# Seven block products for eight in the up-projection of a spectral layer with a feed-forward block

## The chip, the core and the metric

The kernel runs on one core of one Trainium2 chip. The metric is the device time of one execution in microseconds (us), as the median of a few runs on one chip. The engines are named as in the profile: PE is the matrix engine (PEld its weight loads), DVE the vector engine, ACT the scalar engine, POOL the GpSimd engine, SP the engine that issues the DMAs.

## The reference

Two stages, eight batches of 3008 rows and 256 columns, all in fp32:

```python
X = np.fft.rfft(x, axis=1)                       # x: 8 x 3008 x 256
Yr = Xr @ w_r - Xi @ w_i + b_r                   # Xr, Xi: real and imaginary part of X
Yi = Xr @ w_i + Xi @ w_r + b_i
Y  = shrink(Yr) + 1j * shrink(Yi)                # sign(v) * max(|v| - 0.01, 0)
y  = np.fft.irfft(Y, n=3008, axis=1)             # then y as 24064 rows of 256
h  = y @ w_in                                    # 256 -> 2048
out = (h - np.tanh(h)) @ w_out                   # 2048 -> 256
```

## The kernel before

**Number format.** Every matrix operand is split into a high part, rounded to a short mantissa by an ACT cast, and a low part, the fp32 remainder, which DVE subtracts. A product is then three matmuls: high by high, high by low, low by high. These operands have the type fp32r in the program and take one pass. A few matmuls of the transforms have plain fp32 operands and take two passes each, so that the trace counts them twice.

**The spectral stage** works batch by batch. `Forward` multiplies pairs of 94 rows by the first DFT factor (`dft`, L215 to L217), and `keep` copies the result out for a DMA to `a_dram`. `Spectrum` loads it again and applies the second factor (`transform`, L264), the complex product with the weights (`product`, L284, 256 columns wide), the shrinking, and the first factor of the inverse transform (L319 to L321), which goes to `z_dram`.

**The feed-forward stage** works on chunks of `CP = 5` pairs, that is 470 columns (rows of y). `Chunk.time` applies the last inverse factor (L407, 94 columns per pair) and splits its result into `yh` and `yl`. For each of 16 tiles f of 128 features there is then one step:

```python
h   = 6 matmuls: (win_l, yh), (win_h, yh), (win_h, yl), two halves of 256 each   # up, L420
th  = tanh(h)          # ACT,  L423
g   = h - th           # DVE,  L425
gh  = round(g)         # ACT,  L427
gl  = g - gh           # DVE,  L433
o0, o1 += 6 matmuls: (wout_l, gh), (wout_h, gh), (wout_h, gl) for each half      # down, L445
```

The two result banks `o0` and `o1` collect over the 16 steps; `store` copies them out and sends them. There are 52 chunks: 50 of 470 columns and two of 282 at the end. Before the first FFN matmul, batch 0 goes through a special start. The first `FIRST = 3` chunks are interleaved while the fp64 weights `w_in` and `w_out` are converted.

**The order** is written out by hand: every engine runs its instructions in the order of the program. The up matmuls of step g + 2 (`AHEAD = 2`) stand ahead of the down matmuls of step g. The spectral stage of the next batch is put into slots, one slot per step, by `plan_forward`, `plan_spectrum` and `put`; `run(g)` issues what stands in slot g. All DMAs are issued by SP. GpSimd does one subtraction in the whole program (`w2`, L118). PSUM has eight banks of 512 fp32 columns: two for `h`, two for `o`, four (`ps_f`) for the rest.

Of the kernel before, what the change touches and what calls it, by code (L numbers as in the profile page):

```python
# [66 lines left out]
def spectral_ffn(ctx, tc, x, w_r, w_i, b_r, b_i, w_in, w_out, f1, f2, i1, i2, out):  # L67
# [4 lines left out]
    CP = 5  # L72
    CT = CP * 94
# [6 lines left out]
    cvt = ctx.enter_context(tc.tile_pool(name="cvt", bufs=2))  # L80
    ffn = ctx.enter_context(tc.tile_pool(name="ffn", bufs=3))
    dram = ctx.enter_context(tc.tile_pool(name="dram", bufs=2, space=bass.MemoryType.DRAM))
    ps_h = ctx.enter_context(tc.tile_pool(name="ps_h", bufs=2, space=PSUM))
    ps_o = ctx.enter_context(tc.tile_pool(name="ps_o", bufs=1, space=PSUM))
    ps_f = ctx.enter_context(tc.tile_pool(name="ps_f", bufs=4, space=PSUM))

    def split(src, name, pool=const, tag=None, bufs=None, rest=nc.vector):
        hi = pool.tile(list(src.shape), F32R, name=f"{name}_h", tag=f"{tag or name}_h", bufs=bufs)
        lo = pool.tile(list(src.shape), F32R, name=f"{name}_l", tag=f"{tag or name}_l", bufs=bufs)
        nc.scalar.copy(out=hi, in_=src)  # L90
        rest.tensor_tensor(out=lo, in0=src, in1=hi.bitcast(F32), op=ALU.subtract)  # L91
        return hi, lo

# [10 lines left out]
    def linear_loads():  # L104
        wr = ffn.tile([P, 2, D], F32, name="wr_f", tag="g_h")
        wi = load.tile([P, 2, D], F32, name="wi_f", tag="at", bufs=3)
        bias = const.tile([P, 2, D], F32, name="bias")
        yield wr, wi, bias
        for k, v in enumerate((b_r, b_i)):
            yield nc.sync.dma_start(out=bias[:, k, :], in_=v.rearrange("(o e) -> o e", o=1).to_broadcast([P, D]))  # L110
        yield nc.sync.dma_start(out=wi, in_=w_i.rearrange("(t p) e -> p t e", p=P))
        yield nc.sync.dma_start(out=wr, in_=w_r.rearrange("(t p) e -> p t e", p=P))

    def combine_linear(wr, wi, bias, zero):
        w2 = ffn.tile([P, 2, D], F32, name="w2_f", tag="g_h")
        w3 = ffn.tile([P, 2, D], F32, name="w3_f", tag="g_h")
# [30 lines left out]
    def split_f64(part, k, raw):  # L147
# [36 lines left out]
    class Forward:  # L184
# [4 lines left out]
        def load(self):  # L189
            if self.ch == 0:  # L190
                a_dram[self.b] = dram.tile([NP, 96, D], F32, name=f"a_{self.b}", tag="a")
            pool, tag = (load, "xt")
            if self.b == 0:
                pool, tag = ((load, "xt"), (load, "zin"), (work, "yh"), (work, "yl"))[self.ch // 2]
            self.xt = pool.tile([96, XC, D], F32, name="xt", tag=tag)
            nc.sync.dma_start(out=self.xt, in_=x[self.b, :, self.ch * XC:(self.ch + 1) * XC, :])

        def split(self, q, homes=None):
            src, name = self.xt[:94, 2 * q:2 * q + 2, :], f"x_{self.b}_{self.ch}_{q}"
            if homes is None:  # L200
                self.x[q] = split(src, name, work, "sp", 3)
                return
            hi, lo = (
                pool.tile(list(src.shape), F32R, name=f"{name}_{part}", tag=tag, bufs=bufs)
                for part, (pool, tag, bufs) in zip("hl", homes)
            )
            nc.scalar.copy(out=hi, in_=src)
            nc.vector.tensor_tensor(out=lo, in0=src, in1=hi.bitcast(F32), op=ALU.subtract)
            self.x[q] = hi, lo

        def dft(self, q):
            xh, xl = self.x[q]
            self.ps[q] = ps_f.tile([P, 512], F32, name="ps_f1", tag="f")
            pv = self.ps[q][:96].rearrange("p (a d) -> p a d", d=D)
            nc.tensor.matmul(pv, f1h, xl, start=True, stop=False)  # L215
            nc.tensor.matmul(pv, f1l, xh, start=False, stop=False)  # L216
            nc.tensor.matmul(pv, f1h, xh, start=False, stop=True)  # L217
# [26 lines left out]
    class Spectrum:  # L244
        def __init__(self, b, jp):
            self.b, self.jp = b, jp
# [10 lines left out]
        def transform(self):  # L257
            ps = self.ps = ps_f.tile([P, 512], F32, name="ps_f2", tag="f")
# [7 lines left out]
        def dft(self):  # L266
            self.transform()
            ps = self.ps
            self.xh = work.tile([P, 2, 2, P], F32R, name="xh", tag="sp_h", bufs=3)
            self.xl = work.tile([P, 2, 2, P], F32R, name="xl", tag="sp_l", bufs=3)  # L270
# [5 lines left out]
            nc.vector.tensor_tensor(out=self.xl.rearrange(flat), in0=ps, in1=self.xh.bitcast(F32).rearrange(flat), op=ALU.subtract)  # L276
            nc.vector.tensor_tensor(out=xi, in0=pr[:, :, 0, :], in1=xi, op=ALU.add)
# [9 lines left out]
        def cross(self, k):  # L287
            if k == 0:
                self.vv = ps_f.tile([P, 512], F32, name="ps_v", tag="f")
                self.product(self.vv[:, :D], self.xh[:, :, 1], self.xl[:, :, 1], lin[2])  # L290
            else:
                self.product(self.vv[:, D:], self.xh[:, :, 0], self.xl[:, :, 0], lin[1])

        def shared(self):
            t1 = ps_f.tile([P, 512], F32, name="ps_t1", tag="f")
            self.product(t1[:, :D], *self.s, lin[0])
            tb = self.temp("tb", "th")
            nc.vector.tensor_tensor(out=tb, in0=t1[:, :D].unsqueeze(1).to_broadcast([P, 2, D]), in1=bias, op=ALU.add)
# [16 lines left out]
        def inverse(self):  # L315
            zh, zl = self.z
            pz = ps_f.tile([P, 512], F32, name="ps_i1", tag="f")
            pzv = pz.rearrange("p (j e) -> p j e", j=2)
            nc.tensor.matmul(pzv, i1h, zl, start=True, stop=False)  # L319
            nc.tensor.matmul(pzv, i1l, zh, start=False, stop=False)  # L320
            nc.tensor.matmul(pzv, i1h, zh, start=False, stop=True)  # L321
# [7 lines left out]
    class WholeSpectrum(Spectrum):  # L329
        def temp(self, name, tag):  # L330
            return ffn.tile([P, 2, D], F32, name=name, tag=tag)

        def dft(self):
            self.transform()
            self.xf = work.tile([P, 2, 2, P], F32, name="xf", tag="sp_h", bufs=3)
# [37 lines left out]
        def inverse(self):  # L373
            self.pz = ps_f.tile([P, 512], F32, name="ps_i1", tag="f")
            nc.tensor.matmul(self.pz.rearrange("p (j e) -> p j e", j=2), i1f, self.mn, start=True, stop=True)

    total = B * NP
    sizes = [CP] * (total // CP)
    if total % CP:
        sizes = sizes[:-1] + [(CP + total % CP + 1) // 2, (CP + total % CP) // 2]  # L380
    begin = [sum(sizes[:c]) for c in range(len(sizes))]
    NCH = len(sizes)

    FIRST = 3

    class Chunk:
        def __init__(self, c):
            self.c, self.n = c, sizes[c] * 94
            self.pairs = [(p // NP, p % NP) for p in range(begin[c], begin[c] + sizes[c])]

        def load(self):
            self.zt = load.tile([96, CP, D], F32, name="zin", tag="zin")
            k = 0
            while k < len(self.pairs):
                b, p = self.pairs[k]
                n = sum(q[0] == b for q in self.pairs[k:])
                nc.sync.dma_start(out=self.zt[:, k:k + n, :], in_=z_dram[b][p:p + n].rearrange("a p d -> p a d"))
                k += n

        def time(self, t):  # L400
            n = self.n
            if t == 0:
                tags = ("st", "st") if self.c == FIRST - 1 else ("yh", "yl")
                self.yh, self.yl = (work.tile([P, 2, 512], F32R, name=m, tag=g) for m, g in zip(("yh", "yl"), tags))
            ps = ps_f.tile([P, 512], F32, name="ps_i2", tag="f")
            for k, (_, p) in enumerate(self.pairs):
                nc.tensor.matmul(  # L407
                    ps[:, k * 94:(k + 1) * 94], self.zt[:, k, t * P:(t + 1) * P], i2t[:, p * 94:(p + 1) * 94],
                    start=True, stop=True,
                )  # L410
            nc.scalar.copy(out=self.yh[:, t, :n], in_=ps[:, :n])  # L411
            nc.vector.tensor_tensor(out=self.yl[:, t, :n], in0=ps[:, :n], in1=self.yh[:, t, :n].bitcast(F32), op=ALU.subtract)

        def up(self, f):
            n = self.n
            h = ps_h.tile([P, 512], F32, name="h", tag="h")
# [304 lines left out]
```

## Time and profile before

| | |
|---|---|
| median of 3 runs | 2696.31 us (2693.75 to 2697.34) |
| span of the profiled execution, first to last instruction | 2694.1 us |
| granted PE clock, mean of the span | 0.998 |
| PE busy | 2676.7 us, 99% |
| DVE busy | 1748.3 us, 65% |
| ACT busy | 1377.5 us, 51% |
| POOL busy | 2.0 us, 0% |
| HBM traffic | 60 GB/s over the span |

The time of the profiled execution is its span of 2694.1 us and a little around it; the median of the runs is 2.2 us above the span. In a timeline a row shows the start of a group of equal instructions, the time from the start of its first to the end of its last, and the idle time before it with what ended it. Matmuls overlap, since the next one enters while the last drains: what one costs in a stream is the distance from its start to the next start, not its duration.

### The profile page before, as it was taken

The numbers are of one execution on the slowest core, as the hardware profiler recorded it, in microseconds if no ns is written. First come the engines' busy times: TensorE is split into PE (matmuls) and PEld (weight loads), VectorE is DVE, ScalarE is ACT, GpSimd is POOL, SyncE is SP. The second block draws the span as 40 slices with busy tenths as digits, with TensorE's granted clock in tenths as the row PEclk, the third lists the DMA queues.
The fourth block names the chain that finished last, engine by engine and source line by source line (L and its number), as shares of the span: only waits on it lengthen the run. The fifth ranks groups of instructions, "written<-read, shape, count | busy, mean of one in ns | idle before, by whom it ended". The sixth has DMA issues, their size and how long they took to land.

```text
span 2694.1 us, 36955 instructions
## 1 busy us (share of the span) xinstructions
PE 2676.7 (99%) x14169; PEld 2391.6 (89%) x14169; DVE 1748.3 (65%) x3079; ACT 1377.5 (51%) x2587; POOL 2.0 (0%) x5
## 2 busy tenths in 40 slices
PE   8999999999999999999999999999999999999999
PEld 6788988999889998999988999899988999998989
DVE  6895786666557666566755667666665666655555
ACT  5555555454554446454455445644455444444445
POOL 0000000000000000000000000000000000000000
PEclk9999999999999999999999999999999999999999
DMA  6423223110231103111022110411113111100000
GB/s 196 141 75 106 65 83 109 46 54 26 69 90 43 50 32 111 57 47 46 24 81 80 46 46 31 118 56 50 39 39 108 50 39 41 35 23 22 20 20 17
DMA packets 105135, 163.47 MB, mean 61 GB/s; under 512 B 7488, under 2 KB 70976, under 8 KB 104864
## 3 DMA queue, kind: packets, MB, share of 16 engines
q1 hardware_dynamic: 104960, 161.13, 19.8%
q8 instruction: 111, 1.82, 0.3%
q14 instruction: 64, 0.52, 0.1%
HBM read 86.13 MB, written 74.97 MB: 60 GB/s over the span
## 4 chain that ended last, share of the span: by engine, by line
PE 94%; DVE 3%; DMA 1%; ACT 1%; issue 1%; SPq 0%; DVEq 0%; ACTq 0%
PE o L445 37%; PE h L420 37%; PE ps_v L284 4%; PE ps_i L407 4%; PE ps_f L264 3%; PE ps_t L284 2%; PE ps_f L215 1%; PE ps_f L217 1%; PE ps_f L216 1%; PE ps_v L352 1%; DVE g L425 1%; PE ps_i L320 1%; PE ps_i L321 1%; PE ps_i L319 1%; DVE gl L433 0%
## 5 line engine op out<-in xcount | busy, mean ns | idle before, releaser
L425 DVE TENSOR_TENSOR g<-h,th 128x470 f32<-128x470 f32 (+1 forms) x832 | 532.2, 640 | 540.0 <-ACT th L423 531.9
L423 ACT ACTIVATE th<-h 128x470 f32<-128x470 f32 (+1 forms) x832 | 463.9, 558 | 757.3 <-PE h L420 756.3
L433 DVE TENSOR_TENSOR gl<-g,gh 128x470 fp32r<-128x470 f32 (+1 forms) x832 | 531.9, 639 | 285.8 <-ACT gh L427 203.2
L427 ACT CAST gh<-g 128x470 fp32r<-128x470 f32 (+1 forms) x832 | 483.0, 581 | 408.6 <-DVE g L425 401.2
L445 PE MATMUL o<-gh,wout_l 128*128 128x470 f32 (+1 forms) x1664 | 631.3, 379 | 1.1 <-ACT gh L427 1.1
L445 PE MATMUL o<-gl,wout_h 128*128 128x470 f32 (+1 forms) x1664 | 616.1, 370 | 1.1 <-DVE gl L433 1.1
L445 PE MATMUL o<-gh,wout_h 128*128 128x470 f32 (+1 forms) x1664 | 615.8, 370 | 0.0
L420 PE MATMUL h<-yl,win_h 128*128 128x470 f32 (+1 forms) x1664 | 480.7, 370 | 0.0
L420 PE MATMUL h<-yh,win_l 128*128 128x470 f32 (+1 forms) x1664 | 480.1, 370 | 0.0
L420 PE MATMUL h<-yh,win_h 128*128 128x470 f32 (+1 forms) x1664 | 479.5, 369 | 0.0
L445 PEld LDWEIGHTS o<-gl,wout_h 128*128 128x128 f32 x1664 | 312.8, 188 | 40.8 <-DVE gl L433 2.1
L445 PEld LDWEIGHTS o<-gh,wout_l 128*128 128x128 f32 x1664 | 313.1, 188 | 35.1 <-ACT gh L427 1.7
L420 PEld LDWEIGHTS h<-yh,win_l 128*128 128x128 f32 x1664 | 310.5, 188 | 36.2 <-ACT yh L411 0.4
L420 PEld LDWEIGHTS h<-yl,win_h 128*128 128x128 f32 x1664 | 310.6, 188 | 35.5
L420 PEld LDWEIGHTS h<-yh,win_h 128*128 128x128 f32 x1664 | 310.6, 188 | 35.5
L445 PEld LDWEIGHTS o<-gh,wout_h 128*128 128x128 f32 x1664 | 313.5, 188 | 32.0
L309 DVE TENSOR_TENSOR y<-tb,ps_v 64x256 f32<-64x256 f32 x384 | 160.2, 417 | 12.0 <-ACT tb L356 6.8
L407 PEld LDWEIGHTS ps_i<-i,zin 96*128 96x128 f32 x1024 | 126.1, 192 | 5.0 <-DVE st L231 1.0
L407 PE MATMUL ps_i<-i,zin 96*128 96x94 f32 x1024 | 128.0, 272 | 1.0 <-DVE st L231 0.8
L91 DVE TENSOR_TENSOR x_l<-xt,x_h 94x512 fp32r<-94x512 f32 x126 | 85.6, 686 | 46.2 <-ACT x_h L90 44.3
L264 PEld LDWEIGHTS ps_f<-f,at 128*128 128x128 f32 x768 | 101.5, 192 | 13.6 <-issue 8.2
L264 PE MATMUL ps_f<-f,at 128*128 128x128 f32 x768 | 103.1, 277 | 5.7 <-DMA at<-a 5.7
(98 smaller groups left out, 2077.8 us busy)
## 6 DMA issues: line engine op xcount, KB each, us to landing
xt<-in_x SPq DMA_DIRECT2D x64, 384.0 KB, 3.6
at<-a SPq DMA_DIRECT2D x96, 256.0 KB, 2.8
z<-zo SPq DMA_DIRECT2D x96, 256.0 KB, 2.0
out<-ot SPq DMA_DIRECT2D x50, 470.0 KB, 2.9
a<-st SPq DMA_DIRECT2D x56, 384.0 KB, 3.2
zin<-z SPq DMA_DIRECT2D x44, 480.0 KB, 4.2
w_raw<-in_moe_w_in SPq DMA_DIRECT2D x8, 512.0 KB, 4.6
w_raw<-in_moe_w_out SPq DMA_DIRECT2D x8, 512.0 KB, 5.1
```

Of the source, the lines that this page charges most:

```text
L91: rest.tensor_tensor(out=lo, in0=src, in1=hi.bitcast(F32), op=ALU.subtract)
L215: nc.tensor.matmul(pv, f1h, xl, start=True, stop=False)
L264: nc.tensor.matmul(pv[:, t, jj], self.at[:, jj, t * P:(t + 1) * P], rhs, start=True, stop=True)
L284: nc.tensor.matmul(dst, lhs[:, t], rhs[:, t, :], start=n == 0, stop=n == 5)
L309: nc.vector.tensor_tensor(out=y[ri * 64:(ri + 1) * 64, jj, :], in0=common(jj, ri), in1=self.vv[jj * 64:(jj + 1) * 64, ri * D:(ri + 1) * D] ...
L407: nc.tensor.matmul(ps[:, k * 94:(k + 1) * 94], self.zt[:, k, t * P:(t + 1) * P], i2t[:, p * 94:(p + 1) * 94], start=True, stop=True,)
L420: nc.tensor.matmul(h[:, :n], lhs[:, t, f * P:(f + 1) * P], rhs[:, t, :n], start=k == 0, stop=k == 5)
L423: nc.scalar.activation(out=th[:, :n], in_=h[:, :n], func=AF.Tanh)
L425: nc.vector.tensor_tensor(out=g[:, :n], in0=h[:, :n], in1=th[:, :n], op=ALU.subtract)
L427: nc.scalar.copy(out=gh[:, :n], in_=g[:, :n])
L433: nc.vector.tensor_tensor(out=gl[:, :n], in0=g[:, :n], in1=gh[:, :n].bitcast(F32), op=ALU.subtract)
L445: nc.tensor.matmul(self.o[t][:, :n], lhs[:, f, t * P:(t + 1) * P], rhs[:, :n], start=f == 0 and k == 0, stop=f == NF - 1 and k == 2,)
```

## The change

From chunk 3 on (`FIRST`), the up-projection takes two tiles f at once. The weights of the pair are seen as a 2x2 matrix of blocks A (two halves of the 256 inputs by two tiles f), the chunk's y as a 2x2 matrix of blocks B (two halves of the inputs by two halves of the columns), and the product is made with Strassen's seven block products in Winograd's order, not eight. Each block product is three matmuls (high and low parts as before) on half a chunk's columns: 21 matmuls for a pair of tiles where there were 12 on a whole chunk. Besides:

- Chunks have 512 or 480 columns (`widths`), six to a batch, so that 48 chunks replace 52, and the halves have 256 or 240.
- The sums of weight blocks (`sums`, three tiles in high and low parts; a fourth overwrites one block of `win`) are made once, in slots 36 to 53 (`weight_sums`). The sums of y blocks (`t1` to `t4`) are made per chunk: differences on GpSimd (`Chunk.sums`), then seven casts on ACT and seven subtractions on GpSimd (`operands`). The operand tiles have one buffer each.
- The sums of products are made in PSUM. A pair has two banks, `H0` or `H1`: `c11` and `acc` in one, `c21` and `c22` in the other. `keep` has ACT copy `c11` to the tile `p7` (in `late`) and then `acc` to `c11`; `u3` and `low_right` have DVE add `p7` to `acc`. PE waits for each of these, since they touch a bank that it writes next.
- tanh, g, gh and gl work on both tiles at once, 1024 columns (960) wide.
- The remainders of the spectral stage's splits (`x_l`, `s_l`, `z_l`) go from DVE to GpSimd; the product with the low part comes last in their matmuls.
- y is copied raw from PSUM by ACT (`take`), with a spill tile where a chunk border cuts a pair; `Unit` loads and transforms it in pieces of two or three pairs.
- The slots, the tiles' homes and the PSUM banks are laid out anew; the early steps (chunks 0 to 2) keep the six matmuls of `up`, now 512 wide.

In this diff the loop at the end is the new order of the main part; one turn is two slots and one pair of tiles.

```diff
+    widths = [512, 512, 512, 512, 480, 480]
+    def split_into(hi, lo, src, rest=nc.gpsimd):
         nc.scalar.copy(out=hi, in_=src)
         rest.tensor_tensor(out=lo, in0=src, in1=hi.bitcast(F32), op=ALU.subtract)
...
+        def sums(self, k):                        # Chunk
+            b11, b12, b21, b22 = self.halves()
+            sub = lambda o, a, b: nc.gpsimd.tensor_tensor(out=o, in0=a, in1=b, op=ALU.subtract)
+            if k == 0:
+                sub(self.spare(0), b22, b12)
+                sub(b12, b12, b11)
+            elif k == 1:
+                sub(self.spare(1), b22, b12)
+            else:
+                sub(self.spare(0), b21, self.spare(1))
...
+    class Pair:
+        def product(self, dst, left, right, start=False):
+            ah, al = self.left(left)
+            bh, bl = (v[:, :self.m] for v in ys[right])
+            for k, (a, b) in enumerate(((al, bh), (ah, bh), (ah, bl))):
+                nc.tensor.matmul(dst, a, b, start=start and k == 0, stop=k == 2, skip_group_check=True)
+        def phase0(self):
+            self.open()
+            self.product(self.c11, "s3", "t3", True)
+            self.product(self.acc, "a11", "b11")
+        def keep(self):
+            nc.scalar.copy(out=self.p7, in_=self.c11)
+            nc.scalar.copy(out=self.c11, in_=self.acc)
+        def phase1(self):
+            self.product(self.acc, "s2", "t2")
+            self.product(self.c11, "a12", "b21")
+        def u3(self):
+            nc.vector.tensor_tensor(out=self.c21, in0=self.acc, in1=self.p7, op=ALU.add)
+        def phase2(self):
+            self.product(self.acc, "s1", "t1")
+        def low_right(self):
+            nc.vector.tensor_tensor(out=self.c22, in0=self.acc, in1=self.p7, op=ALU.add)
+        def phase3(self):
+            self.product(self.acc, "a21", "b22")
+            self.product(self.c21, "a22", "t4")
...
+        for Q in range(-1, PERIODS + 2):
+            call(Q, "low_right")
+            call(Q - 1, "high")
+            run_later()
...
+            call(Q - 2, "down", 1, 0)
+            call(Q - 1, "low")
+            call(Q + 1, "phase0")
+            call(Q + 1, "keep")
+            run_last()
+            run(sa)
+            run_later()
...
+            call(Q, "phase3")
+            call(Q, "tanh")
+            run_last()
+            call(Q - 2, "down", 1, 1)
...
+            call(Q + 1, "phase1")
+            call(Q + 1, "u3")
+            call(Q, "g")
+            call(Q - 1, "down", 0, 0)
+            run(sb)
+            call(Q - 1, "down", 0, 1)
+            call(Q + 1, "phase2")
```

The order of the built program shows this in three places. On PE before, in the middle of the main part, up (L420) and down (L445) alternate, six matmuls each:

```order
L420 MATMUL h<-yh,win_l 128x470 x2
L420 MATMUL h<-yh,win_h 128x470 x2
L420 MATMUL h<-yl,win_h 128x470 x2
L445 MATMUL o_15868<-gh,wout_l 128x470
L445 MATMUL o_15868<-gh,wout_h 128x470
L445 MATMUL o_15868<-gl,wout_h 128x470
```

On PE after, in the main part near the end of the program, from `phase0` of one pair on (`y_t` and `y_b` are operands t and b, `y_more` holds b22 and t4, `sum` the weight sums):

```order
L576 MATMUL H_2035<-y_t_1981,sum_1_1848 128x256
L576 MATMUL H_2035<-y_t_1981,sum_0_1847 128x256 x2
L576 MATMUL H_2035<-y_b_1982,win_l 128x256
L576 MATMUL H_2035<-y_b_1982,win_h 128x256 x2
L576 MATMUL H_2036<-y_more,win_l 128x256
L576 MATMUL H_2036<-y_more,win_h 128x256 x2
L576 MATMUL H_2036<-y_more,win_l 128x256
L576 MATMUL H_2036<-y_more,win_h 128x256 x2
L505 MATMUL o_25267<-gh,wout_l 128x512
L505 MATMUL o_25267<-gh,wout_h 128x512
L505 MATMUL o_25267<-gl,wout_h 128x512
L576 MATMUL H_2035<-y_t_1984,sum_1_1846 128x256
```

The up matmuls now stand in four groups (`phase0`, `phase3`, `phase1`, and `phase2` further on), with the pair's other bank or one half of a down between those that wait for each other.

On ACT before, a stretch of the main part:

```order
L427 CAST gh<-g 128x470
L423 ACTIVATE th<-h 128x470
L427 CAST gh<-g 128x470
L423 ACTIVATE th<-h 128x470
```

On ACT after, in the last chunks of the main part, with four of the next chunk's operand casts:

```order
L614 CAST gh<-th 128x1024
L584 COPY late<-H_2035 128x256
L585 COPY H_2035<-H_2035 128x256
L607 ACTIVATE th<-H_2036 128x1024
L87 CAST y_t_1981<-late 128x240
L87 CAST y_b_1982<-raw 128x240
L87 CAST y_t_1984<-late 128x240
L87 CAST y_b_1983<-raw 128x240
L614 CAST gh<-th 128x1024
```

The two copies of `keep` come between the cast of one pair and the tanh of the next, and the operand casts ahead of the next cast. On GpSimd, where before there was one subtraction, the operands' differences and remainders stand between those of the spectral stage:

```order
L531 TENSOR_TENSOR late<-raw 128x256
L531 TENSOR_TENSOR raw<-raw 128x256
L88 TENSOR_TENSOR z_0_l<-mn,z_0_h 128x512
L531 TENSOR_TENSOR late<-raw 128x256
L88 TENSOR_TENSOR y_t_1981<-late,y_t_1981 128x256
L88 TENSOR_TENSOR y_b_1982<-raw,y_b_1982 128x256
```

So one remainder of the spectral stage (`z_0_l`) is ahead of a chunk's operands in GpSimd's queue.

More of the change, by code (lines that the diff above doesn't have):

```diff
@@ L373, in inverse @@
         def inverse(self):
-            self.pz = ps_f.tile([P, 512], F32, name="ps_i1", tag="f")
+            self.pz = bank("ps_i1")
             nc.tensor.matmul(self.pz.rearrange("p (j e) -> p j e", j=2), i1f, self.mn, start=True, stop=True)
[L377 to L382, printed above, removed]
-    FIRST = 3
+    widths = [512, 512, 512, 512, 480, 480]
@@ L386, in spectral_ffn @@
+    Unit.turn = 0
     class Chunk:
         def __init__(self, c):
[L388 to L398, printed above, removed]
@@ L400, in time @@
-        def time(self, t):
-            n = self.n
[L402 to L412, printed above, removed]
@@ L461, in spectral_ffn @@
-    slots = {}
-    def put(slot, fn, *a):
-        slots.setdefault(slot, []).append((fn, a))
-    def plan_forward(b, start, each, ahead, first=0):
-        for ch in range(first, NP // XC):
-            f = Forward(b, ch)
-            put(start + ch * each - ahead, f.load)
-            for q in range(XC // 2):
-                put(start + ch * each + q * each // 2, f.part, q)
-    def plan_spectrum(b, start, each, ahead, lag):
+            th, gh, gl = (v[i % 4 // 2][:, i % 2, :n] for v in early_tiles)
@@ new lines, in plan_spectrum, with plan_forward, calmest, prepare @@
+            if shared == cross:
+                busy(k + shared, 9.0)
+    def plan_forward(f, q, slot):
+        put(slot - 1, 2, f.split, q)
+        put(slot, 7, f.part, q)
+        busy(slot, 0.8)
+        busy(slot - 1, 0.1)
+    def calmest(lo, hi, n, us):
+        found = sorted(sorted(range(lo, hi + 1), key=lambda k: (load_at.get(k, 0.0), k))[:n])
+        for k in found:
+            busy(k, us)
+        return found
+    def prepare(c):
+        chunk = chunks[c]
+        at = zero_slot(c)
+        if c > FIRST:
+            put(at - 15, 0, chunk.unspill)
+        put(at - 5, 9, chunk.sums, 0)
+        put(at - 4, 9, chunk.sums, 1)
+        put(at - 3, 1, chunk.operands, "t3", "b11", "t2", "b21")
+        put(at - 2, 1, chunk.operands, "t1")
+        put(at - 2, 9, chunk.sums, 2)
+        put(at - 1, 1, chunk.operands, "b22", "t4")
+        busy(at - 3, 1.0)
+        busy(at - 1, 0.6)
@@ L689, in spectral_ffn, with rise, finish, fall @@
-    for g in range(HELD, len(order)):
-        step(g, lambda: run(g))
+        ready, half = {}, {}
+        def rise(g):
+            if g < len(order):
+                c, f = order[g]
+                half[g] = chunks[c].up(f, g)
+        def finish(g):
+            if g in half:
+                c, f = order[g]
+                ready[g] = chunks[c].rest(*half.pop(g))
+        def fall(g, t):
+            if g in ready:
+                c, f = order[g]
+                chunks[c].down(f, *ready[g], t)
```

593 lines of the change are left out of this document (421 added, 172 removed).

## The prediction

> **What bounds the kernel now.** I read the page's first lines first, then PE's own waits, then a table by stage, and last the timeline of PE, to learn what a matmul costs in a stream.
>
> ```profile
> span 2694.1 us, 36955 instructions
> PE 2676.7 (99%) x14169; PEld 2391.6 (89%) x14169; DVE 1748.3 (65%) x3079; ACT 1377.5 (51%) x2587; POOL 2.0 (0%) x5
> PE 94%; DVE 3%; DMA 1%; ACT 1%; issue 1%; SPq 0%; DVEq 0%; ACTq 0%
> ```
>
> PE is busy for 99% of the span and carries 94% of the chain that ended last. From the waits of PE, longest first, and the busy time by stage (us, then PE, PEld, DVE, ACT, POOL with counts, granted clock, DMA):
>
> ```profile
> PE ps_f L264 <- DMA at<-a: 5.7, 1, 5.7
> PE o L445 <- ACT gh L427: 1.1, 1, 1.1
> 270.00:2690.00 2420.00, 2419.21 (x12977) 2179.04 (x12976) 1549.68 (x2715) 1224.80 (x2307) 0.00 (x0) 1.00 0.18 53
> ```
>
> PE waits for almost nothing, and in the main part it is busy for 2419 of 2420 us at full clock. So the time is the sum of the distances between matmul starts. A change pays what it takes out of that sum, less the new waits that it makes. These groups hold the FFN (count, busy, mean ns):
>
> ```profile
> L445 PE MATMUL o<-gh,wout_l 128*128 128x470 f32 x1600 | 612.6, 383 | 1.1 <-ACT gh L427 1.1
> L420 PE MATMUL h<-yh,win_h 128*128 128x470 f32 x1600 | 466.1, 373 | 0.0
> L420 PE MATMUL h<-yh,win_h 128*128 128x282 f32 x64 | 13.3, 289 | 0.0
> ```
>
> Each of the six groups (three of up, three of down) has 1600 matmuls of 470 columns and 64 of 282. Their mean of 370 to 380 ns is no price, because matmuls overlap. The timeline of PE gives it, from start to start:
>
> ```profile
> 1504.72 0.58 PE L420 MATMUL h<-yl,win_h 128*128 128x470 f32 x2
> 1505.14 0.39 PE L319 MATMUL ps_i<-z_l,i_h 128*128 128x512 f32 x1
> ...
> 1505.83 0.38 PE L445 MATMUL o<-gh,wout_l 128*128 128x470 f32 x1
> ...
> 1507.10 0.58 PE L420 MATMUL h<-yh,win_l 128*128 128x470 f32 x2
> ...
> 1508.37 0.40 PE L284 MATMUL ps_v<-w_h,xl 128*128 128x256 f32 x2
> ...
> 1509.08 0.38 PE L445 MATMUL o<-gh,wout_l 128*128 128x470 f32 x1
> ...
> 1548.05 1.25 PE L407 MATMUL ps_i<-i,zin 96*128 96x94 f32 x10
> 1549.08 0.46 PE L445 MATMUL o<-gh,wout_l 128*128 128x470 f32 x1
> 1549.38 0.37 PE L445 MATMUL o<-gh,wout_h 128*128 128x470 f32 x1
> 2685.40 0.76 PE h L420 x6
> ```
>
> At 470 columns two take 0.42 us (1504.72 to 1505.14): 0.210 each in up; the six of L445 from 1505.83 to 1507.10 take 1.27: 0.2115 in down. At 512 the three of L319 to L321 take 0.69 (1505.14 to 1505.83): 0.230. At 256 the six of L284 take 0.71: 0.118. At 282 six take 0.76 (last line, from the chain of waits): 0.127. At 94 columns, ten passes take 1.03 and the matmul behind them starts its successor 0.09 late (0.30 for 0.21): 0.112 per pass, nearly what 256 columns cost. So there is a floor near 0.11, below which fewer columns gain nothing.
>
> **a) The matmuls of the FFN.** Before: 4800 x 0.210 + 4800 x 0.2115 + 384 x 0.127 = 2072 us. After: chunks 0 to 2 have 288 up matmuls of 512 columns; the other 45 chunks (29 of 512, 16 of 480) have 8 pairs with 21 matmuls each, 4872 of 256 columns and 2688 of 240; down has 3072 of 512 and 1536 of 480. At 480 I take 0.2155, between the rows for 470 and 512. No row shows an fp32r matmul of 240 columns: a line through 470 and 282 gives 0.109, the row at 256 with its scatter 0.119; I take 0.115, nearer to the row that is 16 columns away and above the floor. Sum: 3360 x 0.230 + 1536 x 0.2155 + 4872 x 0.118 + 2688 x 0.115 = 773 + 331 + 575 + 309 = 1988. Change: **-84 us**, between -63 (0.120 and 0.119) and -105 (0.117 and 0.109). One eighth fewer column passes in up would be near -130; the per-matmul part of 21 short matmuls against 12 long ones takes the rest.
>
> The Trainium skill ("TensorE: Matmul & The Clock Gate", section "Back-to-back issue gap") gives N/2.4 + 2.5 ns for the isolated gap. By it 470 columns cost 198 ns, 512 cost 216, 256 cost 109 and 240 cost 102.5, and a) would be -106. This trace disagrees at each width that it shows: 210, 230 and 118 ns.
>
> **b) One turn of the new order.** ACT and DVE now stand between PE's groups, so I lay out one turn (one pair, 512 columns) from rows. Their forms at two widths give a slope, for 1024 columns:
>
> ```profile
> L425 DVE TENSOR_TENSOR g<-h,th 128x470 f32<-128x470 f32 x800 | 517.8, 647 | 534.2 <-ACT th L423 529.4
> L433 DVE TENSOR_TENSOR gl<-g,gh 128x470 fp32r<-128x470 f32 x800 | 517.3, 647 | 271.8 <-ACT gh L427 189.4 <-PE o L445 75.6
> L427 ACT CAST gh<-g 128x470 fp32r<-128x470 f32 x800 | 469.3, 587 | 393.9 <-DVE g L425 386.5
> L423 ACT ACTIVATE th<-h 128x470 f32<-128x470 f32 x800 | 450.9, 564 | 749.6 <-PE h L420 748.6 <-PE ps_f L215 1.0
> L425 DVE TENSOR_TENSOR g<-h,th 128x282 f32<-128x282 f32 x32 | 14.5, 452 | 5.8 <-ACT th L423 2.6
> L427 ACT CAST gh<-g 128x282 fp32r<-128x282 f32 x32 | 13.7, 428 | 14.7 <-DVE g L425 14.7
> L423 ACT ACTIVATE th<-h 128x282 f32<-128x282 f32 x32 | 13.0, 407 | 7.7 <-PE h L420 7.7
> L277 DVE TENSOR_TENSOR xi<-ps_f,xi 128x256 f32<-128x256 f32 x84 | 34.9, 416 | 0.0
> L275 ACT COPY xi<-ps_f 128x256 f32<-128x256 f32 x84 | 32.1, 382 | 0.0
> L90 ACT CAST s_h<-xi 128x256 fp32r<-128x256 f32 x84 | 34.0, 404 | 26.1 <-DVE xi L277 25.2
> 1505.40 0.56 ACT L423 ACTIVATE th<-h 128x470 f32<-128x470 f32 x1 [1.25 <-PE h L420]
> 1505.99 0.65 DVE L425 TENSOR_TENSOR g<-h,th 128x470 f32<-128x470 f32 x1 [0.72 <-ACT th L423]
> ```
>
> tanh: 564 + (564 - 407)/188 x 554 = 1.03 us; in the same way 1.22 for g and for gl, 1.06 for the cast; a copy of `keep` 0.38, `u3` and `low_right` 0.42 each. From PE to ACT it takes 0.26 after the group's last slot (up ends 1505.14, tanh starts 1505.40), from ACT to DVE 0.03 (1505.96 to 1505.99). With t = 0 at the start of the first down half, PE runs: down to 0.69, phase0 to 1.40, phase3 to 2.11, down to 2.80, phase1 to 3.50, two down halves to 4.88, phase2 to 5.24. Then `low_right` runs 0.26 to 0.68 (phase3 wants it at 1.40); the copies 1.66 to 2.45 (phase1 wants them at 2.80); tanh to 3.48; `u3` 3.76 to 4.18 (phase2: 4.88); g to 5.40 (the bank is wanted at 5.93); the cast to 1.25 of the next turn, gl to 2.50 (wanted by the third matmul of the down half that starts at 3.50: 3.96). All are in time; the smallest margin is 0.35 us, of the copies. ACT is busy for 2.85 and DVE for 3.28 of the 5.24, so neither is the bound. Spectral work in a turn lengthens PE's groups, too. The even turn therefore adds **0**.
>
> **c) New waits at borders.** GpSimd takes over the remainders. The trace shows it once, beside a DVE subtraction that starts at the same time (min, median, max in ns, then the start):
>
> ```profile
> L117 DVE SCALAR_TENSOR_TENSOR w_f<-wr_f,wi_f x1: 691/691/691, 25.7 to 25.7; 128x512 f32<-128x512 f32 x1
> L118 POOL TENSOR_TENSOR w_f<-wi_f,wr_f x1: 1770/1770/1770, 25.7 to 25.7; 128x512 f32<-128x512 f32 x1
> ```
>
> The splits of x are, by form:
>
> ```profile
> L90 ACT CAST x_h<-xt 94x512 fp32r<-94x512 f32 x126 | 76.6, 619 | 1.6 <-DMA xt<-in_x 1.4
> L231 ACT COPY st<-ps_f 96x512 f32<-96x512 f32 x121 | 70.4, 582 | 19.1 <-PE ps_f L217 11.9
> ```
>
> 512 columns cost 1.77 us, or 1.08 if the first 0.69 were a wait for DVE; 256 columns half of each, 0.54 to 0.89. Three places can make PE wait. A split stands one slot ahead of its `dft`: a cast of 0.62 behind the copies ends at 3.07, GpSimd at 4.15 to 4.84, the low-part matmul wants it at 4.65: 0 to 0.19, in about half of 96 groups, 0 to 9 us. At a chunk's border `b11`'s remainder ends by 5.66 at the long price and is wanted at 6.5; with one spectral remainder of 1.77 ahead in the queue it is 0.9 late: 0 to 41 us over 45 borders. Batch 1's twelve row groups come in six slots with the weight sums, where ACT has two such casts and copies and half a turn, 2.40 + 1.42 = 3.8 us per slot, against PE's 2.62 + 6 x 0.230 = 4.0: 0 to 8 us. I take **+15** of 0 to 58, low, because each needs the long price and a bad place at once.
>
> **d) Small terms.** The last pair's tanh, g, cast and gl (960 columns) outlast the five down halves left by some 1 us, and the last store is larger: +2 (0 to 4). The 94-column matmuls are the same 512, but come in 188 groups for 104; if the late successor (0.09) is a cost per group, that is 8 us: +3 (0 to 8). The start up to 112 us keeps its work and order: 0, a few us either way. What DVE gives up to GpSimd gains nothing: it was off the chain (3%).
>
> **Sum.** 2694.1 - 84 + 15 + 2 + 3 = 2630 us of span; the median of the runs stands 2.2 above the span: **2632 us**, 2.4% faster. About 0.2% (5 us) is what a measurement of this kernel can tell from no change.
>
> **Rivals.** *The copies are late (slower than before).* PE's phase1 waits for both copies of `keep`, which read and write PSUM on ACT; no row shows ACT writing to PSUM. With phase0 and phase3 ahead, the turn has 0.35 us of margin, and each us beyond it costs 360 turns. Late by 0.53, at 0.65 us per copy for 0.38, the gain of 64 is gone; late by 0.75, PE waits 0.40 a turn: 2632 + 144 = 2776. For it: the chain from copies over tanh and g closes within a turn with few tenths to spare. Against: every row of ACT at 256 columns, casts included, is near 0.4.
>
> *GpSimd and DVE hold each other up.* The pair of rows at 25.7 can be read so that the one that starts second waits for all of the other. Then gl, with a margin of 1.46, can start 1.77 late behind a wide GpSimd operation (108 for x and 84 for z) and cost PE 0.31: at most 60, some 30 in the middle: 2660 (2652 to 2692). The Trainium skill ("SBUF — State Buffer", "Who interferes with whom") states just this lock, for a DVE instruction with two SBUF inputs against a GpSimd one that reads SBUF; the 1.77 beside 0.69 fits it, one sample.
>
> *The narrow form is slow (slower).* All fp32r matmuls of the trace have 256 columns or more; plain fp32 ones take two passes, of 0.215 each at 256 columns (four from 53.63 to 54.49):
>
> ```profile
> 53.63 1.03 PE L352 MATMUL ps_t<-wr_f,sf 128*128 128x256 f32 x4
> 54.49 1.02 PE L375 MATMUL ps_i<-mn,i_f 128*128 128x512 f32 x2
> ```
>
> If fp32r fell back to that below 256 columns, 2688 matmuls would cost 0.40 each for 0.115: +770, 3400 us. Only the gap in the trace's widths leaves room for it.
>
> *The isolated gap rules.* With the page's -106 for -84: 2610 us. The timeline speaks against it.
>
> **How the numbers follow.** Forecast (2612 to 2652) 0.58; the page's gap (2596 to 2612) 0.06; GpSimd and DVE, or the far ends of c) (2652 to 2690) 0.14; waits that just eat the gain 0.05; late copies 0.13; the slow narrow form 0.04. Faster 0.58 + 0.06 + 0.14 = 0.78, same 0.05, slower 0.17. The range 2596 to 2690 holds the first three.
>
> **What would show it.** Right: L576 starts 0.115 to 0.12 apart, both widths; PE over 98% busy; copies of 0.4 us; PE's waits on ACT's copies near 0, those on GpSimd under 20 us. Wrong: a wait of PE for L585 or L592 in each turn; copies over 0.6; gl far behind its cast; a 240-column row with a much larger distance.

## The result and the profile after

The changed kernel takes 2658.76 us (median of 4 runs, 2656.65 to 2660.55); the kernel before took 2696.48 beside it (2693.75 to 2697.34). The ratio is 0.9864 (0.985 to 0.9878): 37.7 us or 1.4% faster. The forecast was 2632 us, so the direction and the range held, and 27 us of the expected gain of 64 did not come. The time lies in the band from 2652 to 2690, to which the prediction gave 0.14, and not in the forecast's own band that ends at 2652.

The profiled execution spans 2654.8 us, 39.3 less than before. First lines of the page, and the shares of the chain that ended last:

```profile
span 2654.8 us, 43312 instructions
PE 2611.6 (98%) x16641; PEld 2343.2 (88%) x16641; DVE 1720.6 (65%) x2613; ACT 1578.9 (59%) x2950; POOL 697.9 (26%) x829
PE 86%; DVE 2%; POOL 1%; ACT 1%; issue 1%; DMA 0%; SPq 0%; POOLq 0%; ACTq 0%; DVEq 0%
```

PE is still the bound. But its share of the chain fell from 94% to 86%, and it now waits for other engines. Its waits (total, times, longest):

```profile
PE ps_f L218 <- POOL x_l L88: 9.8, 7, 1.6
PE ps_f L262 <- DVE y L326: 7.2, 10, 0.7
PE H L576 <- DVE H L592: 3.5, 1, 3.5
PE he L481 <- DVE yl L462: 1.6, 1, 1.6
```

No row names the copies of `keep` (L584, L585). Groups of the new turn:

```profile
L576 PE MATMUL H<-y_t,sum 128*128 128x256 f32 x2088 | 358.4, 280 | 4.1 <-DVE H L592 3.5 <-POOL y_b L88 0.7
L607 ACT ACTIVATE th<-H 128x1024 f32<-128x1024 f32 x232 | 239.6, 1033 | 79.7 <-PE H L576 77.9
L584 ACT COPY late<-H 128x256 f32<-128x256 f32 x232 | 86.8, 374 | 143.1 <-PE H L576 141.0
L585 ACT COPY H<-H 128x256 f32<-128x256 f32 x232 | 82.8, 357 | 7.4
```

The copies take 0.37 and 0.36 us, tanh 1.03, as estimated from the rows before.

**Where the 39.3 us come from.** I added up distances between matmul starts in both traces. Up to the first FFN matmul: 111.92 us before, 119.28 after, **+7.4**. From there to the last FFN matmul: 2578.1 before (to 2690.04), 2530.8 after (to 2650.06), **-47.3**. The tail: +0.7. The stretch of -47.3 is -81 of shorter matmul streams and +34 of pauses. Pauses are counted here as what a distance has beyond the median of its width, where that is over 0.1 us: 39.5 after, 5.6 before.

The pauses have three places. At the end of the special start, from 220 to 300 us, they are some 9 us. While batch 1's columns run, from 325 to 427 us, a column transform starts 0.9 us late ten times and a row transform once. And six times, once per batch, PE stands still for 1.75 us more than the usual 0.23 between L217 and L218. The last kind, around 792 us:

```profile
791.10 0.75 POOL L88 TENSOR_TENSOR y_b<-raw,y_b 128x256 fp32r<-128x256 f32 x1
791.62 1.25 DVE L618 TENSOR_TENSOR gl<-th,gh 128x960 fp32r<-128x960 f32 x1 [0.53 <-ACT gh L614]
791.79 2.19 POOL L88 TENSOR_TENSOR x_l<-xt,x_h 94x512 fp32r<-94x512 f32 x1
792.05 0.40 PE L217 MATMUL ps_f<-x_h,f_h 94*96 94x512 f32 x1
794.03 0.48 PE L218 MATMUL ps_f<-x_l,f_h 94*96 94x512 f32 x1 [1.58 <-POOL x_l L88]
```

`x_l` starts late on GpSimd because four remainders of the chunk's operands (`y_t`, `y_b`) were ahead of it in the queue, and then takes 2.19 us beside gl, where 1.29 is the median.

### The profile page after: what moved, and what is told of

It is laid out like the page before. It is cut to its first block, busy times and chain, and to the rows that moved or that the text cites. A ratio compares the mean times of both kernels' runs of the same rounds, so it can differ in the third digit from the quotient of the medians.

```text
span 2654.8 us, 43312 instructions
## 1 busy us (share of the span) xinstructions
PE 2611.6 (98%) x16641; PEld 2343.2 (88%) x16641; DVE 1720.6 (65%) x2613; ACT 1578.9 (59%) x2950; POOL 697.9 (26%) x829
## 4 chain that ended last, share of the span: by engine, by line
PE 86%; DVE 2%; POOL 1%; ACT 1%; issue 1%; DMA 0%; SPq 0%; POOLq 0%; ACTq 0%; DVEq 0%
PE o L505 36%; PE H L576 32%; PE ps_v L289 4%; PE ps_i L428 4%; PE ps_f L262 3%; PE ps_t L289 2%; PE ps_f L218 1%; PE ps_f L216 1%; PE ps_f L217 1%; DVE y L326 1%; PE ps_i L336 1%; PE ps_i L337 1%; PE ps_i L338 1%; POOL x_l L88 1%; DVE tb L300 0%
## 5 line engine op out<-in xcount | busy, mean ns | idle before, releaser
L576 PEld LDWEIGHTS H<-y_t,sum 128*128 128x128 f32 x3240 | 530.6, 188 | 91.8 <-DVE H L592 3.9
L505 PE MATMUL o<-gh,wout_l 128*128 128x512 f32 (+1 forms) x1440 | 572.5, 398 | 0.1
L505 PE MATMUL o<-gh,wout_h 128*128 128x512 f32 (+1 forms) x1440 | 561.5, 390 | 0.0
L505 PE MATMUL o<-gl,wout_h 128*128 128x512 f32 (+1 forms) x1440 | 560.7, 389 | 0.5 <-DVE gl L618 0.5
L576 PE MATMUL H<-y_t,sum 128*128 128x256 f32 (+1 forms) x3240 | 550.9, 278 | 4.1 <-DVE H L592 3.5
L614 ACT CAST gh<-th 128x1024 fp32r<-128x1024 f32 (+1 forms) x360 | 372.3, 1034 | 281.1 <-DVE th L610 231.4
L618 DVE TENSOR_TENSOR gl<-th,gh 128x1024 fp32r<-128x1024 f32 (+1 forms) x360 | 435.7, 1210 | 48.8 <-ACT gh L614 44.1
L592 DVE TENSOR_TENSOR H<-H,late 128x256 f32<-128x256 f32 (+1 forms) x360 | 153.6, 427 | 450.5 <-PE H L576 407.7
L610 DVE TENSOR_TENSOR th<-H,th 128x1024 f32<-128x1024 f32 (+1 forms) x360 | 429.3, 1192 | 2.4 <-ACT th L607 0.3
L607 ACT ACTIVATE th<-H 128x1024 f32<-128x1024 f32 (+1 forms) x360 | 364.6, 1013 | 108.8 <-PE H L576 105.7
L88 POOL TENSOR_TENSOR z_l<-mn,z_h 128x512 fp32r<-128x512 f32 x84 | 110.3, 1313 | 769.3 <-ACT z_h L87 769.3
L598 DVE TENSOR_TENSOR H<-H,late 128x256 f32<-128x256 f32 (+1 forms) x360 | 153.6, 427 | 242.1 <-PE H L576 235.7
L576 PE MATMUL H<-y_b,win_h 128*128 128x256 f32 (+1 forms) x1440 | 284.7, 279 | 0.0
L584 ACT COPY late<-H 128x256 f32<-128x256 f32 (+1 forms) x360 | 132.8, 369 | 235.5 <-PE H L576 232.6
L576 PE MATMUL H<-y_more,win_h 128*128 128x256 f32 (+1 forms) x1440 | 266.5, 278 | 0.0
L576 PEld LDWEIGHTS H<-y_more,win_h 128*128 128x128 f32 x1440 | 219.0, 189 | 4.4
L576 PEld LDWEIGHTS H<-y_b,win_h 128*128 128x128 f32 x1440 | 219.6, 189 | 0.0
L576 PE MATMUL H<-y_more,win_l 128*128 128x256 f32 (+1 forms) x720 | 209.3, 291 | 0.0
L576 PE MATMUL H<-y_b,win_l 128*128 128x256 f32 (+1 forms) x720 | 200.8, 279 | 0.0
```

What stands on the lines that cost most here:

```text
L505: nc.tensor.matmul(self.o[t][:, :n], lhs[:, f, t * P:(t + 1) * P], rhs, start=f == 0 and k == 0, stop=f == NF - 1 and k == 2,)
L576: nc.tensor.matmul(dst, a, b, start=start and k == 0, stop=k == 2, skip_group_check=True)
L584: nc.scalar.copy(out=self.p7, in_=self.c11)
L592: nc.vector.tensor_tensor(out=self.c21, in0=self.acc, in1=self.p7, op=ALU.add)
L598: nc.vector.tensor_tensor(out=self.c22, in0=self.acc, in1=self.p7, op=ALU.add)
L607: nc.scalar.activation(out=self.th, in_=self.hp[:, :, :n], func=AF.Tanh)
```

## The experiments

Each is the changed kernel with one edit, except the first. The median of before was 2696.38 beside the first four, 2694.62 beside the next four and 2696.04 beside the last two.

**1. The price of a width.** The kernel before, with a stream of matmuls behind its end:

```diff
+for w in (512, 470, 384, 320, 256, 240, 192, 128, 256, 240):
+    for k in range(96):
+        nc.tensor.matmul(pw[:, :w], wout_h[:, k % NF, :P], win_h[:, k % 2, :w], start=True, stop=True)
```

> The kernel before, with ten streams of 96 fp32r matmuls behind its last step, each with new weights, 512, 470, 384, 320, 256, 240, 192, 128, 256 and 240 columns wide; nothing reads their results. Theory: a matmul costs its columns and a small fixed part, but never less than the load of its 128 weight columns, about 0.11 us. Then the distances are 0.23, 0.21, 0.172, 0.144, 0.118, 0.112, and 192 and 128 columns cost 0.105 to 0.112 like 240. Rival one, no floor, only the isolated gap: 192 columns 0.083 and 128 columns 0.056. Rival two, fp32r is slow below 256 columns: 240, 192 and 128 at 0.2 or more (the changed kernel's own 240-column rows at 0.112 already speak against it).

It took 2833.13 us (one run). Groups of the added line (count, busy, mean ns); busy by count is the price:

```profile
L694 PE MATMUL price<-win_h,wout_h 128*128 128x256 f32 x192 | 23.4, 283 | 0.0
L694 PE MATMUL price<-win_h,wout_h 128*128 128x512 f32 x96 | 21.9, 389 | 0.0
L694 PE MATMUL price<-win_h,wout_h 128*128 128x240 f32 x192 | 21.8, 275 | 0.0
L694 PE MATMUL price<-win_h,wout_h 128*128 128x470 f32 x96 | 20.6, 375 | 0.0
L694 PE MATMUL price<-win_h,wout_h 128*128 128x192 f32 x96 | 10.9, 274 | 0.0
L694 PE MATMUL price<-win_h,wout_h 128*128 128x128 f32 x96 | 10.9, 275 | 0.0
```

From start to start the medians are 0.227 at 512, 0.120 at 256, 0.112 at 240, and 0.111 at both 192 and 128. So a floor of 0.111 us is there, 240 columns lie just on it, and nothing falls back to two passes.

**2. A warmer start.** Eight more idle matmuls ahead of the first inverse transform: `idle(6)` becomes `idle(14)`.

> The changed kernel with 14 instead of 6 filler matmuls ahead of the first last-inverse-factor matmuls of batch 0. Its trace shows the PE clock at half from 110.3 to 123.9 us, after a wait of 1.1 us for the load of z, where the kernel before kept the full clock; the first FFN matmul starts 7.4 us later than before. Theory: the pause let the clock fall, and the filler keeps it up: first FFN matmul 4 to 6 us earlier, time 2653 to 2655 against 2658.8. Rival: the start is late because of the load and the splits, not of the clock: the full clock comes back but the first FFN matmul moves by under 1.5 us, time within 2 us.

2659.85 us (2659.58 to 2660.88), ratio 0.9867 (0.9853 to 0.988): no gain. The half-clock period around the first FFN matmul shrank from 13.7 to 3.4 us, but that matmul came only 1.2 us earlier (118.05), and the eight matmuls cost time themselves. The rival held: the start is late because of the load and the splits. Then three other pauses were followed by half-clock periods that the changed kernel has shorter or not at all: 6.8 us at 278 us, 3.4 us at 1435 and at 2077. Against the changed kernel, step by step, the lead of 0.2 us turns into +1.4 after 1435 and +2.9 after 2077. So warmth at the start gave nothing in the end, and a pause can cost more than itself.

**3. A reserve at the border.** The planner holds one more microsecond free in the slot two ahead of each new chunk.

```diff
         put(at - 1, 1, chunk.operands, "b22", "t4")
+        busy(at - 2, 1.0)
```

> The changed kernel with the row transforms of the next batch kept out of the one slot whose split stands behind a chunk's operand casts. In the trace PE waits there for the remainder of x from GpSimd, 1.6 us in each of six batches, behind four operand remainders and one DVE operation with two SBUF inputs. Theory: the wait is a matter of GpSimd's queue at that slot: PE's waits for x_l fall from 9.8 to under 2 us and the time by 8 to 10 us, to about 2650. Rival: GpSimd is late in any slot: the waits move to another slot and the time stays within 2 us of 2658.8.

2654.32 us (2652.4 to 2657.48), ratio 0.9847 (0.9834 to 0.9861). The gain of 4 is half of what I expected, and the two sets of runs overlap. The six long waits did not go: five remain with the same 1.98 us between starts, some 50 us earlier (741, 1061, 1381 ...), where now `z_l` and a `y_t` stand ahead of `x_l` on GpSimd. Moving the slot moved the wait, as the rival said.

**4. Batch 1's columns one slot later.** `plan_spectrum(1, 56, ...)` becomes `plan_spectrum(1, 57, ...)`.

> The changed kernel with batch 1's spectral stage one slot later, so that its column transform falls into the second slot of a turn and not into the first. In the trace the column transform waits 0.7 to 0.9 us in each of ten turns for DVE's last reading of the product's PSUM bank (two banks now, four before). Theory: with a slot more between the product and the next transform the bank is free: PE's waits of this kind (7.2 us) fall to under 1.5 us and the time by 6 to 9, to about 2651. Rival: DVE is simply full in this stage (7.9 us of work in a turn of 8.9): the wait turns up at another place and the time stays within 2 us.

2672.98 us (2667.34 to 2675.08), ratio 0.9911 (0.9898 to 0.9925): 14 us slower than the changed kernel, a miss. Some 5 us of it fall into half-clock periods (462, 1131 and 1773 us). The ten waits of 0.7 for the column transform are gone, and eleven longer ones stand in their place (its waits, then the timeline at one of them):

```profile
PE ps_t L289 <- POOL s_l L88: 16.7, 11, 1.6
PE ps_v L289 <- DVE xl L276: 3.8, 11, 0.4
368.32 1.15 DVE L618 TENSOR_TENSOR gl<-th,gh 128x960 fp32r<-128x960 f32 x1
368.68 1.91 POOL L88 TENSOR_TENSOR z_l<-mn,z_h 128x512 fp32r<-128x512 f32 x1 [9.23 <-ACT z_h L87]
370.56 0.71 POOL L88 TENSOR_TENSOR s_l<-xi,s_h 128x256 fp32r<-128x256 f32 x1
```

In this order `s_l`, which PE wants next, is queued on GpSimd behind the wide `z_l`, which is itself drawn out to 1.91 us (1.30 in the median) by gl on DVE.

**5. The seven products undone, all else kept.** Twelve full-width matmuls per pair of f tiles, `(win_l, yh), (win_h, yh), (win_h, yl)` as before the change (`plain`), from one split of the chunk (`whole`); no copies, additions or operand sums; the new order, chunk widths and GpSimd's part stay.

```diff
-            self.product(self.c11, "s3", "t3", True)
-            self.product(self.acc, "a11", "b11")
+            self.plain(0, 0, 3)
...
-        put(at - 3, 1, chunk.operands, "t3", "b11", "t2", "b21")
...
+        put(at - 4, 1, chunk.whole)
```

> The changed kernel with only the seven-product form undone from the fourth chunk on: twelve full-width matmuls per pair of f tiles instead of twenty-one half-width ones, no copies in keep, no additions in u3 and low_right, no weight or operand sums, one split of the chunk into yh and yl; the new order, the new chunk widths, and GpSimd for the remainders stay. Theory A (the matmul stream is what counts): by the distances measured in the changed kernel (480 columns .219, 240 columns .112, 512 columns .232, 256 columns .118) each pair costs 12 x .219 - 21 x .112 = .28 us more, over 360 pairs +100 us; some of the pauses at borders may go (-5 to -20): 2735 to 2760, that is slower than the kernel before by some 50 us, since the new widths and order alone bring nothing. Rival B (the gain came from the new order and widths, and the seven products bring little): 2660 to 2690.

2735.21 us (2732.78 to 2736.06), ratio 1.0145 (1.0128 to 1.0162). This splits the change in two. The seven products alone are worth 2735.2 - 2658.8 = 76 us, at the lower end of theory A. What came with them, chunks of 512 and 480 columns instead of 470, the new order and GpSimd's part together, costs some 40 us. That cost is in the matmuls, not in waits. The sum of distances over all FFN matmuls is 2092.8 us before and 2132.0 here for the same 2310144 columns in up and as many in down, +39.2. Apart from the start, this kernel has almost no pauses (0.2 us in all, counted as above, between 300 and 2640). Per column the 470-wide matmul had the better price: 0.210 for 470 is 0.447 ns, 0.233 for 512 is 0.455; the means are 0.453 and 0.462. In the changed kernel up takes 956.0 instead of 1065.5, -109.5 us. Of these, 26.7 come back as pauses by the count that gives 0.2 here, and some 6 in the hand-over (PE is busy for 185.2 us between 112 and 300 us here, 179.1 in the changed kernel).

**6. All remainders on DVE.** The default of the splits' last argument, in three places: `rest=nc.gpsimd` becomes `rest=nc.vector`.

> The changed kernel with every split remainder on DVE instead of GpSimd (829 instructions moved, POOL nearly empty). DVE would grow from 1721 us to about 2070 us (78%), by .41 us for 240 columns and .66 to .75 for 512. Theory A (TensorE's pauses behind GpSimd and its lock with DVE are about 11 us, and DVE has room): 2645 to 2655. Rival B (DVE's one queue becomes the next wait: additions and remainders of batch 1's columns stand behind each other): 2665 or more. If GpSimd were the bound of the whole stretch, 2620.

2679.91 us (2677.77 to 2684.16), ratio 0.9944 (0.9929 to 0.9959). Rival B's time came, but not at its place: of the loss, some 3 us lie in batch 1's columns. 607 of the 829 instructions moved, the operand differences stayed on GpSimd, and DVE is at 74%, so it is not full. But at the chunks' borders four operand remainders now stand in its one queue ahead of `low_right` (L598). PE's longest sum of waits, and one of them:

```profile
PE H L576 <- DVE H L598: 17.5, 20, 1.1
1551.17 0.79 POOL L531 TENSOR_TENSOR late<-raw,late 128x256 f32<-128x256 f32 x1 [14.99 <-DVE y_t L88]
1551.28 0.96 DVE L88 TENSOR_TENSOR y_t<-late,y_t 128x256 fp32r<-128x256 f32 x1
1552.17 0.41 DVE L88 TENSOR_TENSOR y_b<-raw,y_b 128x256 fp32r<-128x256 f32 x1
1552.50 0.42 DVE L598 TENSOR_TENSOR H<-H,late 128x256 f32<-128x256 f32 x1
1552.97 0.38 PE L576 MATMUL H<-y_more,win_l 128*128 128x256 f32 x1 [0.94 <-DVE H L598]
```

One `y_t` takes 0.96 for 0.42, because GpSimd started a sum first.

**7. Late copies.** The first copy of `keep` three times, so that the second ends 0.74 us later in all 360 turns.

```diff
-            nc.scalar.copy(out=self.p7, in_=self.c11)
+            for _ in range(3):
+                nc.scalar.copy(out=self.p7, in_=self.c11)
```

> The changed kernel with the copy from c11 to p7 in keep issued three times instead of once, so that the pair's second copy ends two copies (.74 us) later in each of 360 turns; ACT grows by 266 us to about 69%. The output is the same. Theory A (the margins of the trace after: under .5 us in about 80 of 360 turns, more than .8 us in the others): +26 us, 2675 to 2700. Rival B (the even turn as I laid it out, with .35 us of margin in every turn): .39 us in each of 360 turns, +140 us, 2790 to 2800. Rival C (the copies are covered anyway): within 5 us of 2659.

2718.16 us (2716.68 to 2719.45), ratio 1.0084 (1.0069 to 1.0099): +59 against the changed kernel, between A and B. The copies now hold PE up, with a wait row of their own:

```profile
PE H L576 <- ACT H L586: 21.9, 81, 0.4
1503.70 1.18 ACT L585 COPY late<-H 128x256 f32<-128x256 f32 x3 [0.25 <-PE H L576]
1504.92 0.36 ACT L586 COPY H<-H 128x256 f32<-128x256 f32 x1
1505.33 0.62 PE L576 MATMUL H<-y_t,sum 128*128 128x256 f32 x3 [0.27 <-ACT H L586]
```

The 81 turns are those in which nothing else stands between the copies and phase1, and the margin there was 0.3 to 0.5 us, as in my even turn. In distances they lose 34 us in 80 turns at the entry of phase1, 0.43 in each. Some 10 us are spread over 87 other places of L576, the waits for `x_l` go from 9.8 to 14.6, and some 6 us fall into half-clock periods, three of them new (455, 482, 1134 us). By the margins alone I had counted only the first sum, as 26.

**8. Only x on DVE.** Of all remainders, those of x alone move, 108 of 94 x 512:

```diff
-        put(slot - 1, 2, f.split, q)
+        put(slot - 1, 2, f.split, q, None, nc.vector)
```

> The changed kernel with the remainders of the planned row groups' x (x_l, 94 x 512, 88 or so of them from the fourth chunk on) on DVE instead of GpSimd; all other remainders stay on GpSimd. Theory A (the pauses at the six batch borders, 1.75 us each, and two or three in the hand-over are x_l queued behind other remainders on GpSimd): they go, -8 to -13 us, 2646 to 2651. Rival B (x_l is then late behind DVE's own additions, or the pause goes to the next remainder in the queue): 2655 to 2662.

2645.24 us (2642.41 to 2647.23), ratio 0.9813 (0.9798 to 0.9828): 13.5 us faster than the changed kernel. `x_l` takes 0.69 on DVE for 1.29 on GpSimd, and PE waits for it no more. The place of the old wait:

```profile
787.66 1.22 DVE L88 TENSOR_TENSOR x_l<-xt,x_h 94x512 fp32r<-94x512 f32 x1
788.28 1.20 POOL L88 TENSOR_TENSOR y_b<-raw,y_b 128x256 fp32r<-128x256 f32 x1
789.24 0.39 PE L217 MATMUL ps_f<-x_h,f_h 94*96 94x512 f32 x1
789.47 0.39 PE L218 MATMUL ps_f<-x_l,f_h 94*96 94x512 f32 x1
```

The two still lengthen each other here (1.22 and 1.20), but neither is late. The wait of 3.5 us for L592 in the hand-over shrank to 0.5.

**9. One addition earlier.** On top of 8, in batch 1 the addition of the bias (`tb`, 0.68 us) is issued ahead of `low_right`, where DVE stood idle.

```diff
+            while to_add:
+                to_add.pop().common()
             call(Q, "low_right")
```

> x_l on DVE as in e5_xall, and in batch 1's columns the addition of the bias to the common product (tb, .68 us on DVE) is issued ahead of the pair's low_right, where DVE stands idle for some 1.3 us, instead of behind it. Nothing else moves. Theory A (the ten pauses of .9 us in batch 1 are the column transform waiting for a PSUM bank that DVE's additions free last): each pause is .6 to .7 us shorter, -6 to -7 us against e5_xall, 2637 to 2640. Rival B (tb waits for its product there and holds up low_right, so that the pause comes back at the pair's tanh): within 2 us of e5_xall or slower, 2643 to 2650.

2635.71 us (2634.62 to 2638.33), ratio 0.9781 (0.9768 to 0.9795), the fastest version. The kernel of 8 ran beside it once more:

> The kernel of e5_xall once more, beside e9_tb on the same chip: 2642 to 2648.

It took 2644.91 us (2643.63 to 2647.12), so the edit gives 9.2 us, more than the 7 expected. Busy times from 300 to 430 us, PE first, of the kernel of 8 (its second profile) and of this one:

```profile
300.00:430.00 130.00, 121.29 (x821) 109.06 (x821) 95.04 (x163) 71.19 (x142) 40.97 (x48) 1.00 0.18 57
300.00:430.00 130.00, 128.49 (x869) 115.33 (x868) 102.39 (x174) 77.17 (x152) 40.65 (x47) 1.00 0.21 66
```

PE works for 7.2 us more of this stretch. Laid beside the first profile of 8, matmul by matmul, twelve pauses between 318 and 427 us are shorter by 0.70 to 0.74 each, 8.6 us in all: theory A had counted only the ten of the column transform.

## Why the prediction was right, and where it fell short

**a) The matmuls, -84: right in kind, and nearly in size in part by luck.** L576 starts 0.118 us apart at 256 columns and 0.112 at 240 (medians). At 240 the truth lay below the 0.115 taken. Down costs 0.233 at 512 (0.230 predicted) and 0.218 at 480 (0.2155). With these, 3360 x 0.233 + 1536 x 0.218 + 4872 x 0.118 + 2688 x 0.112 = 1994, against 1988: -78 for -84. What I did not see is that the term mixes a loss and a gain. By my prices the new chunk widths cost +3 (2 x (3072 x 0.230 + 1536 x 0.2155) = 2075 for 2072) and the seven products give -87. Experiment 5 shows +39 for the widths and the order, and -109 in up for the seven products. Both were too small in my sum, and the two errors partly cancel: that is the luck. The isolated gap that the prediction took from the Trainium skill ("TensorE: Matmul & The Clock Gate", "Back-to-back issue gap") is out for these matmuls: it gives 0.216 at 512 and 0.103 at 240, and the stream of experiment 1 has 0.227 and 0.112.

**b) The even turn, 0: right.** Durations, order and the smallest margin (the copies) came out as laid out. The rival of late copies was priced too simply: delayed by 0.74 us they cost 59 us, not 0.39 in each of 360 turns, because in three turns of four spectral or border work separates them from phase1.

**c) New waits, +15: the mis-sized term.** With d) and the 94-column groups I had +20; the pauses measured are +34. The 10.5 us at the batch borders come from a place that I named, but the other way round: I let an operand remainder wait behind a spectral one, but PE waits for a spectral one, `x_l`, behind four operand remainders. At that border GpSimd's queue is the cause (experiment 8), and keeping one slot free did not cure it (experiment 3). The ten waits of the column transform are not among my places at all. They come from PSUM: two banks serve the transform and both products, and DVE's additions release them late (experiment 9).

The 9 us of the hand-over lie in my third place, batch 1's row groups beside the weight sums (0 to 8), but not on ACT, where I had priced it. The longest wait, 3.48 us, is for `u3` (L592) on DVE. It stands there behind weight sums that wait for GpSimd:

```profile
276.43 0.73 POOL L88 TENSOR_TENSOR sum<-ws,sum 128x256 fp32r<-128x256 f32 x1
277.19 1.48 DVE L631 TENSOR_TENSOR ws<-ws,ws 128x256 f32<-128x256 f32 x1 [3.13 <-POOL sum L88]
278.71 2.05 DVE L628 TENSOR_TENSOR ws<-win_h,win_l 128x256 f32<-128x256 f32 x1
280.68 0.42 DVE L592 TENSOR_TENSOR H<-H,late 128x256 f32<-128x256 f32 x1
```

On GpSimd the `sum` of 276.43 comes behind two `x_l`; with x on DVE (experiment 8) the wait is 0.5.

**The start, 0: wrong, +7.4.** I took it to keep its work. The first chunk is now 512 columns wide and needs 48 matmuls of 94 columns before its split; before, 40 ran and the first FFN matmul followed. Timelines of before (first three rows) and after:

```profile
106.39 3.59 PE L407 MATMUL ps_i<-i,zin 96*128 96x94 f32 x30
110.79 1.35 PE L407 MATMUL ps_i<-i,zin 96*128 96x94 f32 x10 [0.81 <-DVE st L231]
111.92 0.67 PE L420 MATMUL h<-yh,win_l 128*128 128x470 f32 x2
...
108.57 9.09 PE L428 MATMUL ps_i<-i,zin 96*128 96x94 f32 x48 [1.14 <-DMA zin<-z]
118.87 0.27 DVE L462 TENSOR_TENSOR yl<-ps_i,yh 128x104 fp32r<-128x104 f32 x1 [0.31 <-ACT yh L461]
119.28 1.19 PE L481 MATMUL he<-yh,win_l 128*128 128x512 f32 x2 [1.62 <-DVE yl L462]
```

The 48 take 0.19 each, since most of them fall into a half-clock period of 13.7 us (110.3 to 123.9), and the split now has narrow pieces, cast and subtracted one behind the other. The clock is the smaller part. In the profile of experiment 9 the same 48 start at 108.61 and run at full clock, 0.12 each, and the first FFN matmul still comes at 118.08, because PE then waits longer for the split:

```profile
PE he L485 <- DVE yl L466: 2.9, 1, 2.9
```

So about 1.2 us of the 7.4 are clock, as in experiment 2. Some 2.2 are the later start of the 94-column matmuls (108.57 for 106.39), and the rest is the longer chain.

**GpSimd and DVE hold each other up: true, but rarely on the path.** The Trainium skill ("SBUF — State Buffer", "Who interferes with whom") says that a DVE instruction with two SBUF inputs and a GpSimd one that reads SBUF exclude each other. The runs agree: `x_l` 2.19 beside gl for 1.29, `z_l` 1.91 for 1.30, `y_t` on DVE 0.96 for 0.42, while g and `low_right`, with one input in PSUM, keep their 1.22 and 0.43. Its place was not gl, as I priced it, but `x_l` and `s_l`, which PE wants soonest.

## What to carry to other kernels

Split a change into its arithmetic and what it drags along before adding up: here a gain of 109 us in the up matmuls came with a loss of 39 from the new widths and order, and only a run with one of them undone shows it. When work moves to a slower engine with one queue, ask for each item who wants it first; moving the one that PE wants soonest (13.5 us) beat moving all (-21) and beat moving slots (4 and -14). A wait for a shared PSUM bank is cured at its release: one 0.68 us addition issued in an idle gap gave 9 us.

## What was unexpected of the hardware

The half-clock periods, but for the one that the end of the run cuts, come in multiples of 3.41 us. The same pause of about 1.6 us before L218 passed without loss six times in the changed kernel, and was followed by 3.4 us of half clock twice in experiment 2 and twice in experiment 4. The Trainium skill ("TensorE: Matmul & The Clock Gate", "What's actually happening") gives a free-running window of 3413 ns and says that the clock falls after at least one idle window; the length agrees, but here a pause of half a window sufficed at times.

A 512-column matmul costs 0.227 us in the bare stream of experiment 1 and 0.233 among the FFN's other work, 470 columns 0.210 or 0.216 in the bare stream and 0.210 in the kernel before. Per column the bare stream has 512 as the cheaper one (0.443 ns in the mean, against 0.454 for 470), so width alone does not explain the 39 us. Why the wide ones lose more in company stays open.
